# Spectral mixing followed by a squared-ReLU FFN: batch 0 and the filter loaded over all 128 partitions, products of batch 0 summed in TensorE, batch 1's steps moved to later slots

## The chip, the cores and the metric

The kernel runs on one core of a Trainium2 chip. The metric is device time of one execution in microseconds (us), median over several executions. A span that a trace gives is a little shorter than that time (846.0 against 848.0 for the kernel before), so times of kernels are compared with times and spans with spans. In this kernel TensorE does the matrix products and leaves them in PSUM; VectorE and ScalarE copy results out of PSUM ("evict" them), and with GpSimd cast, copy and multiply; SyncE and ScalarE issue the DMAs, the transfers between DRAM and the memory on chip, which the DMA engines carry out.

## The reference, cut to what matters

```python
# x (8, 3008, 256), filt_r and filt_i (1505, 256), w_in (256, 2048), w_out (2048, 256), all float32
X = np.fft.rfft(x, axis=1)
Y = X * (filt_r + 1j * filt_i)[None, :, :]
y = np.fft.irfft(Y, n=3008, axis=1).astype(np.float32)
h = np.maximum(y.reshape(24064, 256) @ w_in, 0.0)
out = (h * h @ w_out).astype(np.float32)
```

The length 3008 is split as 64 x 47. A forward transform is stage A (47-point sums, on the rows as they were loaded), a transposition through DRAM (`u` is written, `ut` read back), and stage B (64-point sums). VectorE multiplies the result by the filter. Stage P is the inverse 64-point step, `z` goes through DRAM, and stage Y is the inverse 47-point step. The feed-forward part (FFN) then takes 512 tokens at a time. I call one pass of its inner loop a **slot**. Batch 0's transform runs alone in a prologue; each later batch's transform is spread over the slots of the batch before it.

## The kernel before

Its prologue loads x of batch 0 over 94 of 128 partitions, in four chunks, and the filter in eight pieces, half of them with the rows in reverse order:

```python
    def load_f(k, im, rev, q):
        c0, c1 = 12 * k, 12 * k + 12
        r0 = 64 * im + 32 * rev
        v = (filt_i if im else filt_r)[0:1504, :].rearrange("(k1 k2) d -> k1 k2 d", k2=47)
        if rev:
            a = max(c0, 1)
            q.dma_start(out=f32s[k][r0:r0 + 32, a - c0:12, :], in_=v[:, 47 - a:47 - c1:-1, :])
        else:
            q.dma_start(out=f32s[k][r0:r0 + 32, :, :], in_=v[:, c0:c1, :])
```

One unit of stage B computes a product with the filter's real and imaginary parts, swaps the halves of the second one on GpSimd, adds, and gives the sum to stage P:

```python
        nc.vector.tensor_mul(out=prod, in0=ps..., in1=sF[:, :, 2 * p:2 * p + 2, :])
        yf = p_yf.tile([128, 2, D], F16, tag="yf", name=f"yf_{b}_{p}")
        swap = nc.gpsimd if b < 2 else nc.vector
        swap.tensor_copy(out=yf[0:64], in_=prod[64:128, 1])
        swap.tensor_copy(out=yf[64:128], in_=prod[0:64, 1])
    # unit_s:
        nc.vector.tensor_add(out=yf, in0=prod[:, 0], in1=yf)
    # ... (unit_p: two matmuls of yf with sSP, ScalarE evicts, z is written)
```

The write of `u` in the prologue is issued by ScalarE, and there are three `u` buffers for four chunks. The plan of batch 1 puts product and sum of unit p into slots 15 + p and 16 + p (the sum ahead of the next product on VectorE), the reads of z at slot 29, and stage Y from slot 32 on.

## Time and profile before

| | before |
|---|---|
| median of 3 executions | 848.01 us (847.49 to 848.17) |
| profiled span, mean granted TensorE clock | 846.0 us, 0.996 |
| TensorE busy, share of the span | 766.5 us, 91% |
| last eviction of stage P of batch 0 | 70.8 us |
| first FFN matmul | 83.58 us |
| slot 15, slot 30, slot 40 start | 110.40, 153.67, 181.17 us |

The last three rows are from the timeline. They divide the span into the parts that the change can touch: prologue, 15 slots with stage A of batch 1 (which it leaves alone), 15 slots with stage B of batch 1, 10 slots with z and Y of batch 1. What follows, from 181 us to the end, is 665 us that TensorE fills.

### The profile page before, as it was taken

To read this page: it belongs to the slowest core of one execution; us is meant where nothing else is said; L and a number is where in the kernel's file an instruction comes from. 1 tells how busy PE (TensorE), PEld (TensorE's weight loads), DVE (VectorE), ACT (ScalarE), POOL (GpSimd) and SP (SyncE) were. 2 spreads that over 40 slices of the span, in tenths; PEclk is the share of its full clock that TensorE was granted. 3 is DMA by queue.
4 is the path that set the end of the run, shared out by engine and by line. 5 is a ranking of instruction groups with operands and counts; after the bars stand their busy time and mean duration, and the time that the engine had idled before them with its cause. 6 is when DMAs were issued, how large, how long until landed. Compare 5 with 4: busy or idle time off the path is not lost.

```text
span 846.0 us, 13875 instructions
## 1 busy us (share of the span) xinstructions
PE 766.5 (91%) x5760; PEld 531.1 (63%) x5760; DVE 550.4 (65%) x876; ACT 548.7 (65%) x694; POOL 54.2 (6%) x66
## 2 busy tenths in 40 slices
PE   3224887699999999999999999999999999999998
PEld 0112454476677767677767767677767767676666
DVE  4444766455995579755995579755995579543332
ACT  2323755476777767776777767776777767766663
POOL 1186034000000000000000000000000000000000
PEclk9999999899999999999999999999999999999999
DMA  9946544625454245715453345715543332411111
GB/s 242 329 183 169 156 142 126 175 63 169 141 145 115 84 146 149 208 44 169 144 144 112 90 142 153 201 45 167 148 137 114 91 141 75 132 38 39 38 38 50
DMA packets 90799, 109.86 MB, mean 130 GB/s; under 512 B 4120, under 2 KB 80888, under 8 KB 86264
## 3 DMA queue, kind: packets, MB, share of 16 engines
q1 hardware_dynamic: 82256, 100.32, 39.6%
q10 hardware_dynamic: 8384, 8.62, 3.7%
q8 instruction: 45, 0.74, 0.4%
q14 instruction: 18, 0.15, 0.1%
q0 software_dynamic: 96, 0.04, 0.0%
HBM read 59.15 MB, written 49.81 MB: 129 GB/s over the span
## 4 chain that ended last, share of the span: by engine, by line
PE 82%; DMA 7%; DVE 4%; POOL 3%; issue 1%; ACT 1%; ACTq 0%; POOLq 0%; DVEq 0%; SPq 0%
PE psO L371 37%; PE psH L356 36%; DVE prod L275 3%; PE psA L234 3%; PE psY L326 2%; PE psP L298 2%; PE psB L272 2%; DMA f<-in_filt_i_dram 2%; DMA dZ<-ze 1%; POOL yf L281 1%; DMA x<-in_x_dram 1%; POOL yf L282 1%; POOL sF L446 1%; PE psA L252 1%; DMA sSA<-cSA 1%
## 5 line engine op out<-in xcount | busy, mean ns | idle before, releaser
L360 ACT ACTIVATE h<-psH 128x1024 f16<-128x1024 f32 x376 | 384.9, 1024 | 194.1 <-PE psH L356 192.4
L371 PE MATMUL psO<-sWout,h 128*128 128x256 f16 x3008 | 389.5, 273 | 0.0
L356 PE MATMUL psH<-yt,sWin 128*128 128x512 f16 (+7 forms) x1728 | 387.9, 352 | 0.7 <-ACT h L360 0.3
L371 PEld LDWEIGHTS <-h 128*128 128x128 f16 x3008 | 291.3, 98 | 77.2 <-issue 0.6
L364 DVE TENSOR_TENSOR h<-h 128x1024 f16<-128x1024 f16 x376 | 254.2, 685 | 106.0 <-ACT h L360 105.7
L356 PEld LDWEIGHTS <-sWin 128*128 128x128 f16 x1728 | 160.0, 98 | 103.7 <-issue 5.1
L275 DVE TENSOR_TENSOR prod<-psB,sF 128x1024 f16<-128x1024 f32 x96 | 116.9, 1219 | 4.7 <-PE psB L272 4.0
L300 ACT CAST ze<-psP 128x512 f16<-128x512 f32 x96 | 56.2, 585 | 53.9 <-PE psP L298 51.9
L335 DVE CAST yt<-psY 128x376 f16<-128x376 f32 x64 | 35.1, 549 | 69.7 <-PE psY L326 69.4
L241 DVE CAST u<-psA 96x512 f16<-96x512 f32 x56 | 38.4, 686 | 47.8 <-PE psA L234 47.7
L298 PE MATMUL psP<-yf,sSP 128*128 128x256 f16 x192 | 39.5, 290 | 26.9 <-DVE yf L288 15.9
L288 DVE TENSOR_TENSOR yf<-prod,yf 128x512 f16<-128x512 f16 x96 | 40.8, 425 | 30.7 <-POOL yf L282 28.0
L378 ACT COPY ost<-psO 128x512 f32<-128x512 f32 x94 | 55.4, 590 | 6.8 <-PE psO L371 6.0
L326 PE MATMUL psY<-sSY,zt 96*128 96x94 f16 x512 | 43.2, 215 | 13.3 <-DMA zt<-dZ 13.2
L272 PE MATMUL psB<-ut,sSB 128*128 128x256 f16 x192 | 39.0, 289 | 17.9 <-DMA ut<-dU 11.9
L326 PEld LDWEIGHTS <-zt 96*128 96x128 f16 x512 | 36.4, 104 | 29.6 <-DMA zt<-dZ 15.4
L219 DVE CAST x<-x 94x2048 f16<-94x2048 f32 (+1 forms) x36 | 39.2, 1098 | 10.8 <-DMA x<-in_x_dram 10.8
L272 PEld LDWEIGHTS <-sSB 128*128 128x128 f16 x192 | 19.6, 102 | 41.6 <-issue 17.6
L234 PE MATMUL psA<-x,sSA 94*96 94x512 f16 x112 | 42.3, 382 | 2.1 <-DVE u L241 1.3
L298 PEld LDWEIGHTS <-sSP 128*128 128x128 f16 x192 | 17.3, 100 | 36.1 <-DVE yf L288 18.9
L333 ACT CAST yt<-psY 128x376 f16<-128x376 f32 x64 | 29.8, 468 | 14.1 <-PE psY L326 7.4
L239 ACT CAST u<-psA 96x512 f16<-96x512 f32 x56 | 32.1, 574 | 0.0
(28 smaller groups left out, 143.4 us busy)
## 6 DMA issues: line engine op xcount, KB each, us to landing
out_dram<-ost SPq DMA_DIRECT2D x94, 256.0 KB, 3.7
x<-in_x_dram SPq DMA_DIRECT2D x26, 768.0 KB, 6.1
dU<-u SPq DMA_DIRECT2D x28, 384.0 KB, 3.4
dZ<-ze SPq DMA_DIRECT2D x28, 384.0 KB, 2.7
zt<-dZ SPq DMA_DIRECT2D x28, 384.0 KB, 4.6
ut<-dU SPq DMA_DIRECT2D x8, 1024.0 KB, 5.9
ut<-dU SPq DMA_DIRECT2D x8, 512.0 KB, 3.9
x<-in_x_dram SPq DMA_DIRECT2D x4, 640.0 KB, 6.0
```

The costliest lines, as they stand in the source:

```text
L234: nc.tensor.matmul(ps[0:96, :], sSA, x16s[(b, c)][:, 2 * i:2 * i + 2, :], start=True, stop=True)
L272: nc.tensor.matmul(ps[:, i * D:(i + 1) * D], sSB[:, 2 * p + i, :], uts[b][:, 2 * p + i, :], start=True, stop=True)
L275: nc.vector.tensor_mul(out=prod, in0=ps.rearrange("p (a d) -> p a d", d=D).unsqueeze(1).to_broadcast([128, 2, 2, D]), in1=sF[:, :, 2 * p:2 ...
L288: nc.vector.tensor_add(out=yf, in0=prod[:, 0], in1=yf)
L298: nc.tensor.matmul(ps[:, i * D:(i + 1) * D], sSP[:, 2 * p + i, :], prod[:, i, :], start=True, stop=True)
L300: nc.scalar.copy(out=zes[(b, c)][:, 2 * i6:2 * i6 + 2, :], in_=ps.rearrange("p (a d) -> p a d", d=D))
L326: nc.tensor.matmul(ps[:, 94 * jj:94 * jj + 94], zt[:, 4 * (g % 2) + jj, dt * 128:(dt + 1) * 128], sSY, start=True, stop=True)
L356: nc.tensor.matmul(ps[:, i, o:o + n], sWin[:, dt, jt * 128:(jt + 1) * 128], yts[b][:, dt, r:r + n], start=(dt == 0), stop=(dt == 1))
L360: nc.scalar.activation(out=h2[:, 2 * s:2 * s + 2, :], in_=ps, func=AF.Relu)
L364: nc.vector.tensor_mul(out=v, in0=v, in1=v)
L371: nc.tensor.matmul(pso[g][:, t % 2, :], h2s[g][:, jt, t * 128:(t + 1) * 128], sWout[:, jt, :], start=(jt == 0), stop=(jt == NJT - 1))
L378: nc.scalar.copy(out=ost, in_=pso[g])
```

## The change

Its intent is a shorter prologue and a batch 1 in which VectorE no longer waits for GpSimd. x of batch 0 comes in three loads over all 128 partitions in rows of 8 KB (a second set of stage-A weights sorts this out). Each filter part comes in one load of 128 partitions with rows of 12 KB, and casts on ScalarE, GpSimd and VectorE put the pieces into place. In batch 0 the swap and the sum vanish: stage P accumulates both products in PSUM with two weight sets. In batch 1 the sum moves behind the slot's second matmul group, and P, z and Y one slot later.

```diff
-    load_f(0, 1, 0, nc.scalar)        # ... and seven more, reversed rows among them
+    for k, filt in enumerate((filt_r, filt_i)):
+        t = p_y.tile([128, 12, D], F32, tag="yt", name=f"f32_{k}")
+        src = bass.AP(tensor=filt.tensor, offset=filt.offset,
+                      ap=[[12 * D, 4], [47 * D, 32], [1, 12 * D]])
+        nc.sync.dma_start(out=t, in_=src)
...
+                for v, w in enumerate((sSP, sSPx[0])):        # unit_p, b == 0
+                    nc.tensor.matmul(ps[:, i * D:(i + 1) * D], w[:, c2, :], prod[:, v, i, :],
+                                     start=(v == 0), stop=(v == 1))
...
-            put(r + (b == 1), 0, unit_s, b, p)
-            put(r + 2, 1, unit_p, b, p)
+            put(r + (b == 1), b == 1, unit_s, b, p)
+            put(r + 2 + (b == 1), 1, unit_p, b, p)
...
-            put(29 if b == 1 else 35, 1, read_z, b, c)
+            put(30 if b == 1 else 35, 1, read_z, b, c)
-            put((32 if b == 1 else 39) + n // 2, n % 2, unit_y, b, n)
+            if b == 1:
+                r, k = divmod(n, 3) if n < 6 else divmod(n - 2, 2)
+                put(33 + r, min(k, 1), unit_y, b, n)
+            else:
+                put(39 + n // 2, n % 2, unit_y, b, n)
```

More of the change, by code (lines that the diff above doesn't have):

```diff
@@ L31, in _build_consts @@
             SA[:, h, h, 1, c] = np.sin(2 * np.pi * n2 * c / N2)
+    S0 = np.zeros((128, 6, 2, 48))
+    for h in range(2):
+        q = SA[:, h, h].reshape(N2, 48)
+        for t in range(2):
+            S0[2 * h + t::4, t, h] = q[:32]
+        for c in range(4):
+            S0[4 * h + c:120:8, 2 + c, h] = q[32:]
     freq = np.full((NC, 64), -1)
@@ L39, in _build_consts @@
                 freq[c, 32 + j] = 47 * j + 47 - c
-    freq[0, 32] = N // 2
+    freq[0, 63] = N // 2
     SB = np.zeros((NM, 2, 2, NC, 2, 64))
@@ L57, in _build_consts @@
                 SB[:, h, 1, c, 1, f] = -sg * np.cos(th)
-            if c == 0 and f == 32:
+            if c == 0 and f == 63:
                 SB[:, :, 1, c, :, f] = 0.0
@@ L77, in _build_consts @@
     f16 = lambda a, p: np.ascontiguousarray(a.reshape(p, -1).astype(np.float16))
-    return f16(SA, 94), f16(SB, 128), f16(SP, 128), f16(SY, 96)
+    C0 = np.zeros((128, 864))
+    C0[:, 0:576] = S0.reshape(128, 576)
+    C0[0:94, 576:672] = SA.reshape(94, 96)
+    C0[0:96, 672:766] = SY.reshape(96, 94)
+    return f16(C0, 128), f16(SB, 128), f16(SP, 128)
 @with_exitstack
@@ L100 @@
     assert NG * TG == T
-    SA_np, SB_np, SP_np, SY_np = _build_consts()
-    dSA = nc.inline_tensor(SA_np, name="cSA")
+    C0_np, SB_np, SP_np = _build_consts()
+    dC0 = nc.inline_tensor(C0_np, name="cC0")
     dSB = nc.inline_tensor(SB_np, name="cSB")
     dSP = nc.inline_tensor(SP_np, name="cSP")
-    dSY = nc.inline_tensor(SY_np, name="cSY")
     const = ctx.enter_context(tc.tile_pool(name="const", bufs=1))
@@ L154, in load_x @@
         x32s[(b, c)] = t
-    sSA = const.tile([94, 96], F16, name="sSA")
-    nc.gpsimd.dma_start(out=sSA, in_=dSA.ap())
+    sC0 = const.tile([128, 864], F16, name="sC0")
+    nc.scalar.dma_start(out=sC0, in_=dC0.ap())
+    s0 = sC0[:, 0:576].rearrange("p (w q) -> p w q", q=96)
+    sSA = sC0[0:94, 576:672]
+    sSY = sC0[0:96, 672:766]
+    x0 = []
+    v0 = xrows[0:2048, :].rearrange("(p m) d -> p m d", m=16)
+    v1 = xrows[2048:3072, :].rearrange("(p m) d -> p m d", m=8)
+    for k, v in enumerate((v0[:, 0:8, :], v1, v0[:, 8:16, :])):
+        t = (p_h2 if k == 2 else p_x32).tile([128, 8, D], F32, tag="h2" if k == 2 else "x32",
+                                             name=f"x0_{k}")
+        nc.sync.dma_start(out=t, in_=v)
+        x0.append(t)
@@ L161 @@
+    f32s = []
+    for k, filt in enumerate((filt_r, filt_i)):
[3 more added lines that the diff above has]
+        nc.sync.dma_start(out=t, in_=src)
+        f32s.append(t)
     sSB = const.tile([128, NC, 128], F16, name="sSB")
+    nc.sync.dma_start(out=sSB, in_=dSB.ap().rearrange("p (a b) -> p a b", b=128))
     sSP = const.tile([128, NC, 128], F16, name="sSP")
-    sSY = const.tile([96, 94], F16, name="sSY")
+    nc.sync.dma_start(out=sSP, in_=dSP.ap().rearrange("p (a b) -> p a b", b=128))
@@ L166 @@
     sF = const.tile([128, 2, NC, D], F16, name="sF")
-    f32s = [p_y.tile([128, 12, D], F32, tag="yt", name=f"f32_{k}") for k in range(2)]
-    nc.gpsimd.memset(f32s[0][32:64, 0, :], 0.0)
-    nc.gpsimd.memset(f32s[0][96:128, 0, :], 0.0)
-    nc.gpsimd.dma_start(out=f32s[0][32:33, 0, :], in_=filt_r[1504:1505, :])
-    nc.gpsimd.dma_start(out=sSY, in_=dSY.ap())
-    def load_f(k, im, rev, q):
-        c0, c1 = 12 * k, 12 * k + 12
-        r0 = 64 * im + 32 * rev
-        v = (filt_i if im else filt_r)[0:1504, :].rearrange("(k1 k2) d -> k1 k2 d", k2=47)
-        if rev:
-            a = max(c0, 1)
-            q.dma_start(out=f32s[k][r0:r0 + 32, a - c0:12, :], in_=v[:, 47 - a:47 - c1:-1, :])
-        else:
-            q.dma_start(out=f32s[k][r0:r0 + 32, :, :], in_=v[:, c0:c1, :])
@@ L183, with cast_f @@
-    load_x(0, 0)
-    load_f(0, 1, 0, nc.scalar)
-    load_x(0, 1)
-    load_f(0, 1, 1, nc.scalar)
-    load_x(0, 2, p_h2, "h2")
-    load_x(0, 3, p_h2, "h2")
-    load_f(0, 0, 0, nc.sync)
-    load_f(0, 0, 1, nc.sync)
-    nc.sync.dma_start(out=sSB, in_=dSB.ap().rearrange("p (a b) -> p a b", b=128))
+    def cast_f(im, q, eng):
+        o = 64 * im + 32 * (q // 2)
+        c0 = (0, 12, 12, 0)[q]
+        src = f32s[im][32 * q:32 * q + 32, :, :]
+        if q >= 2:
+            src = src[:, ::-1, :]
+        dst = sF[o:o + 32, im, c0:c0 + 12, :]
+        if eng is nc.scalar:
+            eng.mul(out=dst, in_=src, mul=-1.0 if im else 1.0)
+        elif im:
+            eng.tensor_scalar_mul(out=dst, in0=src, scalar1=-1.0)
+        else:
+            eng.tensor_copy(out=dst, in_=src)
@@ L193, with cross_f @@
+    def cross_f(im, k):
+        c = slice(12 * k, 12 * k + 12)
+        if im:
+            nc.vector.tensor_scalar_mul(out=sF[0:64, 1, c, :], in0=sF[64:128, 1, c, :],
+                                        scalar1=-1.0)
+        else:
+            nc.vector.tensor_copy(out=sF[64:128, 0, c, :], in_=sF[0:64, 0, c, :])
     sWin = const.tile([128, 2, DFF], F16, name="sWin")
@@ L213, with cast_x @@
     x16s, us, uts, prods, zes, zts, yts = {}, {}, {}, {}, {}, {}, {}
-    def cast_x(b, c, parts=1):
+    def cast_x(b, c):
         t = p_x16.tile([94, 8, D], F16, tag="x16", name=f"x16_{b}_{c}")
-        n = 8 // parts
-        for k in range(parts):
-            nc.vector.tensor_copy(out=t[:, n * k:n * k + n, :],
-                                  in_=x32s[(b, c)][0:94, n * k:n * k + n, :])
-        x32s.pop((b, c))
+        nc.vector.tensor_copy(out=t, in_=x32s.pop((b, c))[0:94])
         x16s[(b, c)] = t
@@ L243, in unit_a, with chunk_a0 @@
             write_u(b, c, nc.sync)
-    def chunk_a(b, c):
-        us[(b, c)] = p_u.tile([96, 8, D], F16, tag="u", name=f"u_{b}_{c}")
+    def chunk_a0(c):
+        us[(0, c)] = p_u.tile([96, 8, D], F16, tag="u", name=f"u_0_{c}")
         for k in range(2):
-            ps = psH(f"psA_{b}_{c}_{k}")
+            ps = psH(f"psA_0_{c}_{k}")
             for i in range(2):
-                m = 4 * k + 2 * i
-                nc.tensor.matmul(ps[0:96, i, :], sSA, x16s[(b, c)][:, m:m + 2, :],
-                                 start=True, stop=True)
-            o = us[(b, c)][:, 4 * k:4 * k + 4, :]
+                m = slice(4 * k + 2 * i, 4 * k + 2 * i + 2)
+                nc.tensor.matmul(ps[0:96, i, :], s0[:, c // 2, :], x016[2 * (c % 2)][:, m, :],
+                                 start=True, stop=False)
+                nc.tensor.matmul(ps[0:96, i, :], s0[0:120, 2 + c, :], x016[1][0:120, m, :],
+                                 start=False, stop=True)
+            o = us[(0, c)][:, 4 * k:4 * k + 4, :]
             pv = ps[0:96].rearrange("p t (a d) -> p (t a) d", d=D)
@@ L259, in chunk_a @@
                 nc.vector.tensor_copy(out=o, in_=pv)
-        write_u(b, c, nc.scalar)
+        write_u(0, c, nc.scalar)
     def read_u(b):
@@ L278, in unit_b @@
             in1=sF[:, :, 2 * p:2 * p + 2, :])
-        yf = p_yf.tile([128, 2, D], F16, tag="yf", name=f"yf_{b}_{p}")
-        swap = nc.gpsimd if b < 2 else nc.vector
-        swap.tensor_copy(out=yf[0:64], in_=prod[64:128, 1])
-        swap.tensor_copy(out=yf[64:128], in_=prod[0:64, 1])
-        prods[(b, p)] = prod, yf
+        prods[(b, p)] = prod
+        if b > 0:
+            yf = p_yf.tile([128, 2, D], F16, tag="yf", name=f"yf_{b}_{p}")
+            swap = nc.gpsimd if b == 1 else nc.vector
+            swap.tensor_copy(out=yf[0:64], in_=prod[64:128, 1])
+            swap.tensor_copy(out=yf[64:128], in_=prod[0:64, 1])
+            prods[(b, p)] = prod, yf
     def unit_s(b, p):
@@ L289, in unit_s @@
         prods[(b, p)] = yf
+    sSPx = []
     def unit_p(b, p):
@@ L297, in unit_p @@
         for i in range(2):
-            nc.tensor.matmul(ps[:, i * D:(i + 1) * D], sSP[:, 2 * p + i, :], prod[:, i, :],
-                             start=True, stop=True)
+            c2 = 2 * p + i
+            if b == 0:
+                for v, w in enumerate((sSP, sSPx[0])):
+                    nc.tensor.matmul(ps[:, i * D:(i + 1) * D], w[:, c2, :], prod[:, v, i, :],
+                                     start=(v == 0), stop=(v == 1))
+            else:
+                nc.tensor.matmul(ps[:, i * D:(i + 1) * D], sSP[:, c2, :], prod[:, i, :],
+                                 start=True, stop=True)
         nc.scalar.copy(out=zes[(b, c)][:, 2 * i6:2 * i6 + 2, :],
@@ L413, in fft_plan @@
         for n in range(16):
-            put((32 if b == 1 else 39) + n // 2, n % 2, unit_y, b, n)
+            if b == 1:
+                r, k = divmod(n, 3) if n < 6 else divmod(n - 2, 2)
+                put(33 + r, min(k, 1), unit_y, b, n)
+            else:
+                put(39 + n // 2, n % 2, unit_y, b, n)
         return plan
@@ L419, in run, with cast_x0 @@
             f(*a)
-    for c in range(4):
-        cast_x(0, c, 2)
-        chunk_a(0, c)
+    x016 = [p_x16.tile([128, 8, D], F16, tag="x16", name=f"x016_{k}") for k in range(3)]
+    def cast_x0(k, i, copy):
+        m = slice(4 * i, 4 * i + 4)
+        copy(out=x016[k][:, m, :], in_=x0[k][:, m, :])
+    for k in range(2):
+        for i in range(2):
+            cast_x0(k, i, nc.vector.tensor_copy)
+    chunk_a0(0)
+    chunk_a0(2)
+    for i in range(2):
+        cast_x0(2, i, nc.scalar.copy)
@@ L425 @@
+    chunk_a0(1)
+    chunk_a0(3)
     read_u(0)
-    for im in range(2):
-        for rev in range(2):
-            load_f(1, im, rev, nc.scalar)
-    nc.sync.dma_start(out=sSP, in_=dSP.ap().rearrange("p (a b) -> p a b", b=128))
     load_w()
-    nc.scalar.copy(out=sF[0:64, 0, 0:12, :], in_=f32s[0][0:64])
-    nc.vector.tensor_scalar_mul(out=sF[64:128, 1, 0:12, :], in0=f32s[0][64:128], scalar1=-1.0)
-    nc.vector.tensor_scalar_mul(out=sF[0:64, 1, 0:12, :], in0=sF[64:128, 1, 0:12, :], scalar1=-1.0)
@@ L434 @@
-    nc.vector.tensor_copy(out=sF[64:128, 0, 0:12, :], in_=sF[0:64, 0, 0:12, :])
-    for r in range(15):
+    for q in (0, 3):
+        cast_f(0, q, nc.scalar)
+    for q in (1, 2):
+        cast_f(0, q, nc.gpsimd)
+    for q in (0, 3):
+        cast_f(1, q, nc.vector)
+    for q in (1, 2):
+        cast_f(1, q, nc.scalar)
+    sSPx.append(p_x32.tile([128, NC, 128], F16, tag="x32", name="sSPx"))
+    for k in range(2):
+        c = slice(12 * k, 12 * k + 12)
+        nc.gpsimd.tensor_copy(out=sSPx[0][0:64, c, :], in_=sSP[64:128, c, :])
+        nc.gpsimd.tensor_copy(out=sSPx[0][64:128, c, :], in_=sSP[0:64, c, :])
@@ L436 @@
+    for k in range(2):
+        for im in range(2):
+            cross_f(im, k)
+    for r in range(14):
         if r < 12:
             unit_b(0, r)
-        if 1 <= r < 13:
-            unit_s(0, r - 1)
-        if r >= 3:
-            unit_p(0, r - 3)
-        if r in (1, 3):
-            h = r // 2
-            nc.scalar.copy(out=sF[64 * h:64 * h + 64, 0, 12:24, :], in_=f32s[1][0:64])
-        if r == 1:
-            nc.gpsimd.tensor_scalar_mul(out=sF[64:128, 1, 12:24, :], in0=f32s[1][64:128],
-                                        scalar1=-1.0)
@@ L448 @@
-        if r == 4:
-            nc.vector.tensor_scalar_mul(out=sF[0:64, 1, 12:24, :], in0=sF[64:128, 1, 12:24, :],
-                                        scalar1=-1.0)
+        if r >= 2:
+            unit_p(0, r - 2)
+    cast_w()
     for c in range(4):
@@ L454 @@
         load_x(1, c, q=nc.scalar)
-    cast_w()
     for n in range(16):
```

## The prediction

> **What bounds the kernel now.** I read the page first, its 40 slices above all.
>
> ```profile
> span 846.0 us, 13875 instructions
> PE   3224887699999999999999999999999999999998
> DMA  9946544625454245715453345715543332411111
> ```
>
> A slice is 21 us. From the ninth on (170 us) TensorE is 90% busy or more: nothing in the change can shorten that part. All that can be won lies in the first eight slices: the prologue (batch 0's transform, TensorE 20 to 40% busy) and the first forty slots of the feed-forward, which also carry batch 1's transform. Next I read the chain of waits in order of time, for the prologue:
>
> ```profile
> 20.58 1.95 PE psA L252 x4
> ...
> 30.18 13.91 DMA f<-in_filt_i_dram
> 44.13 0.13 issue
> 44.26 7.96 POOL sF L446
> 52.23 0.05 issue
> ...
> 53.90 1.22 DVE prod L275
> ```
>
> Columns: start, duration, what. The filter's second half lands at 44.1, and then GpSimd takes 7.96 us to cast it, with its swaps for stage B queued behind. The timeline adds the rest: stage A runs from 9.0 to 23.8; the intermediate read back (ut) lets stage B start at 34.47; the first five products are out by 40.8, then VectorE idles 12.7 us; in the settled part a product and its sum take 1.58 us a unit; the last eviction of stage P ends at 70.8; the feed-forward starts at 83.58. So the end of P fixes the start of the feed-forward, 12.8 us later.
>
> Then the views by stretches, for the DMA (last two numbers: busy share of the 16 engines, GB/s):
>
> ```profile
> 12.00:14.00 2.00, 1.12 (x3) 0.59 (x4) 1.42 (x3) 0.00 (x0) 0.00 (x0) 1.00 1.04 274
> 46.00:48.00 2.00, 0.00 (x0) 0.00 (x0) 0.00 (x0) 0.00 (x0) 2.00 (x1) 1.00 1.09 387
> ```
>
> The queues are saturated in both, but rows of 1 KB in reverse order beside 8 KB ones give 274, the plain weights 387 (24.2 per engine). Last, the timeline of TensorE and VectorE in the batch-1 stage:
>
> ```profile
> 116.61 1.03 PE L356 MATMUL psH<-yt,sWin 128*128 128x512 f16 x4
> 119.70 0.39 PE L298 MATMUL psP<-yf,sSP 128*128 128x256 f16 x2 [0.97 <-DVE prod L275]
> 119.93 1.03 PE L356 MATMUL psH<-yt,sWin 128*128 128x512 f16 x4
> 121.39 0.43 DVE L288 TENSOR_TENSOR yf<-prod,yf 128x512 f16<-128x512 f16 x1 [1.16 <-POOL yf L282]
> 157.14 1.03 PE L356 MATMUL psH<-yt,sWin 128*128 128x512 f16 x4
> 163.78 0.49 PE L326 MATMUL psY<-sSY,zt 96*128 96x94 f16 x4 [5.61 <-DMA zt<-dZ]
> ```
>
> L356 marks each slot's start. Slots here take 3.31 us (116.61 to 119.93) though TensorE's own work is 2.2: VectorE waits in order for GpSimd's swap before the next product. Later TensorE waits 5.61 us for the read of z.
>
> **What the Trainium skill says.** (1) "DMA: Bandwidth & Descriptors", section "Why a DMA increments its semaphore by 16 and not by 1": a DMA runs on the largest k up to 16 engines that divides the outermost dimension of both its access patterns. The new filter load has a hand-made source pattern whose outermost dimension is 4 (12 rows x 32 x 4). So it gets **four engines, not sixteen**. Nothing in the trace of before shows a large load with such a shape. (2) Same page, "Queues, rings and completion order": every engine serves its queues in turn, packet by packet. The trace agrees: the first write of u, issued at 12.31 beside filled queues, is still awaited at 22.09, while the last, issued at 23.91, had landed by 27.6. (3) "TensorE: Matmul & The Clock Gate", "Back-to-back issue gap": columns/1.2 ns cold, columns/2.4 plus 2.5 ns warm. The trace agrees: 512 columns are 0.43 us apart in stage A and 0.22 in the feed-forward.
>
> **The change part by part.**
>
> *x of batch 0* over 128 partitions: the same 3.1 MB in rows of 8 KB. At an estimated 365 GB/s (between 350 and 389 seen from 40 to 50 us) it has landed by 12 instead of about 18.
>
> *Stage A* needs 32 matmuls instead of 16: cold 8 x 0.43 = 3.4 us a chunk, in place of the 3.86 us that VectorE's cast, wait and eviction cost. Start near 9.7, end near 26 if nothing blocks it. No gain. But there are three u buffers: the fourth chunk waits for the first write of u.
>
> *Filter on four engines.* Each of these moves 3.15 MB / 4 = 786 KB of it; at an estimated 25 GB/s (24.2 was seen per engine) 31.4 us. After x at 11.0 that gives 42.4, with u's packets in between 44. Behind it in the ring lie sSB and sSP (98 KB per engine, 4 us) and the rest of u's writes (135 rows per engine, estimated at 27 ns each: a write of u in the quiet batch-1 stage lands in 3.1 us, some 1.3 of it for 48 rows; 3.6 us): 51.7. Receipt 1.5, read of ut 3.5: stage B can start at 56.7; if the writes get through early and the read queues directly, at 54.6. I take **56**. The casts end close by: ScalarE is held by chunk four until some 41, then four casts at 2.75 us and a cross copy on VectorE: 53.5.
>
> *Stages B and P* lose the 12.7 us stall, the swaps and the sum. VectorE needs 1.17 us a unit (two products took 2.35). TensorE needs two B and four P matmuls of 256 columns, 1.29 us cold, half of it warm. Five units cold and seven at VectorE's pace: 6.5 + 8.2 = 14.6, plus 1.3 for the last P and eviction: 15.9 us instead of 36.3. P ends at 56 + 15.9 = 71.9 against 70.8. **Prologue: 1.1 us later.** The gain of the quicker B is spent on the filter that arrives later. The w casts lie beside that; the weights (behind ut, about 16 us) are there by 70 and cast by 75.
>
> *Batch 1* is the real gain. The sum moves behind the second matmul group of its slot, so the product no longer stands behind the swap. A swap takes about 1.7 us from the product's end (0.94 + 0.61 and gaps), and its sum comes a slot of 2.2 us later. VectorE's own work per slot is 1.14 + 0.34 + 0.60 = 2.1 us by start-to-start distances, below TensorE's 2.2. Slots 15 to 29: before 110.40 to 153.67 = 43.3 us; after, 3 at 1.96, 9 at 2.2 and 3 at 1.96: 31.7. Saved 11.6. Slots 30 to 39: before 153.67 to 181.17 = 27.5. After: ten slots at 1.735, 16 Y units at 0.165, and a remaining wait: z's write, now clear of the x load, lands 3.8 us after slot 30 starts, its read 3.3 later, so 7.3 with issue, against 6.1 at which Y wants it: 1.2 to 1.5. Sum 21.5, saved 6.0. Allowing a little for VectorE at 95%: **17 us saved**.
>
> Sum: 848.0 - 17 + 1.1 = 832.1; I say 832.5.
>
> **The rivals.** *A: the filter does run on all engines.* For it: the author must have meant it so. Then 9.6 MB are in by 29 us, ScalarE's 11 us of casts become the wait before B (the fourth chunk waits for u until about 27, casts to 39), B starts at 40.5, P ends at 56.4, and the total is 848 - 17 - 14.4 = 817. Against it: the rule above; I give 12%. *B: four engines do worse than 24 to 25 GB/s each, or the starved u writes take longer.* At 20 GB/s the filter takes 39 us and B starts at 64: 840. Nothing in the profile speaks on four engines alone; 15%. *C: VectorE and GpSimd get into each other's way in batch 1.* The swap's first half takes 0.94 to 1.01 us beside VectorE and 0.60 alone; two VectorE operations now fall beside it, so that it could come to 1.4 and the sum would just wait. Slots at 2.6 instead of 2.2 give back 5 us: 837. *D: four-engine rate at the top (27 GB/s) and u through early:* B at 53, 829.
>
> **Range and chances.** Main branch 832.5 with a spread of about 4 (rate of an engine, remaining wait for z), and 12% near 817. The 2% line is 831.05, just below the main branch, so this is close: faster 0.42, same 0.56, slower 0.02. Range 818 to 839.
>
> **What would show it.** In the changed profile: DMA share of 0.25 to 0.4 from about 15 to 42 us with near 100 GB/s (four engines of sixteen); the filter loads taking over 12 us each; the fourth chunk's eviction waiting for a u write until nearly 40; stage B from about 56 and 1.2 to 1.3 us a unit without GpSimd; feed-forward start at 85 against 83.6; slots 18 to 26 at 2.2 us; TensorE waiting for z under 2 us. I am wrong if the share stays near 1 until B starts (then rival A), if B's units take over 1.4 us, or if the batch-1 slots still wait for GpSimd.

## The result, and the profile after

The changed kernel takes **852.88 us** (median of 4, 851.58 to 854.47) against 847.84 us for the kernel before on the same chip. The ratio is 1.006, 95% interval 1.0038 to 1.0082: within 2%, but slower, not faster. Ratios here are the mean time of one kernel's fast runs over that of the other's of the same rounds, so they are not quite the ratio of the medians that I quote.

The first view of the page, the one with 40 slices of 21 us, for the kernel after:

```profile
span 849.5 us, 13895 instructions
PE   3105699899999999999999999999999999999998
DMA  9328955545455245815455235815454242511111
```

Before, the DMA row began 9946; now it begins 932. In the second and third slices the DMA engines are busy for 30 and 20% of the time, and TensorE for 10 and 0%. The time went there. The view by stretches of the changed kernel says how much moved (after the stretch's length come busy us of PE, PEld, DVE, ACT and POOL, then clock, DMA share, GB/s):

```profile
10.00:12.00 2.00, 1.95 (x5) 0.97 (x5) 0.60 (x1) 0.47 (x1) 0.00 (x0) 1.00 1.13 369
28.00:32.00 4.00, 0.00 (x0) 0.00 (x0) 0.00 (x0) 0.00 (x0) 0.00 (x0) 0.50 0.27 86
44.00:48.00 4.00, 0.00 (x0) 0.00 (x0) 0.00 (x0) 0.00 (x0) 0.00 (x0) 0.50 0.26 102
```

A share of 0.26 is four engines of sixteen. The chain of waits in order of time (start, duration, what) shows what that cost:

```profile
14.55 38.93 DMA dU<-u
...
54.91 2.02 ACTq L255
...
56.98 2.76 ACT sF L213
59.75 2.77 ACT sF L213
...
68.17 0.95 DVE sF L222
69.15 1.94 DVE prod L307 x2
```

The first write of u is out for 38.93 us. The fourth chunk needs its buffer and can't be evicted before it. Only after that does ScalarE come to its four filter casts, VectorE to the cross copies, and the products start at **69.15**. ScalarE's timeline adds a detail (an ACTq row is the engine's sequencer at an issue of a DMA):

```profile
23.01 16.48 ACTq L255 DMA_DIRECT2D dU<-u  x1
53.56 1.01 ACT L289 CAST u<-psA 96x1024 f16<-96x1024 f32 x1 [32.26 <-DMA dU<-u]
```

The issue of the third write alone held ScalarE's sequencer for 16.48 us, where the first two took 0.35 and 0.32.

For batch 1, VectorE's timeline in a slot of the kernel before (first three lines) and of the kernel after (next four):

```profile
118.42 1.22 DVE L275 TENSOR_TENSOR prod<-psB,sF 128x1024 f16<-128x1024 f32 x1
119.56 0.68 DVE L364 TENSOR_TENSOR h<-h 128x1024 f16<-128x1024 f16 x1
121.74 1.22 DVE L275 TENSOR_TENSOR prod<-psB,sF 128x1024 f16<-128x1024 f32 x1
```

```profile
142.53 1.21 DVE L307 TENSOR_TENSOR prod<-psB,sF 128x1024 f16<-128x1024 f32 x1
143.66 0.41 DVE L322 TENSOR_TENSOR yf<-prod,yf 128x512 f16<-128x512 f16 x1
144.00 1.09 DVE L406 TENSOR_TENSOR h<-h 128x1024 f16<-128x1024 f16 x1
145.01 1.21 DVE L307 TENSOR_TENSOR prod<-psB,sF 128x1024 f16<-128x1024 f32 x1
```

Product to product was 3.32 us and is 2.48. The wait for the swap is gone, but VectorE is now busy without a gap: the FFN's square (`h<-h`) takes 1.09 us instead of 0.68. Later, TensorE (first line) and SyncE's issues at the read of z:

```profile
168.50 0.50 PE L368 MATMUL psY<-sC,zt 96*128 96x94 f16 x4 [3.85 <-DMA zt<-dZ]
```

```profile
157.12 0.33 SPq L163 DMA_DIRECT2D x<-in_x_dram  x1
157.54 0.39 SPq L422 DMA_DIRECT2D out_dram<-ost  x1
159.23 0.32 SPq L346 DMA_DIRECT2D dZ<-ze  x1
164.56 2.38 SPq L353 DMA_DIRECT2D zt<-dZ  x4
```

From the start of each part in both timelines (slots counted by their first-group matmuls: in the kernel after, slot 15 starts at 124.22, slot 30 at 158.42, slot 40 at 185.24) comes this account of the profiled spans:

| part | before, us | after, us | difference |
|---|---|---|---|
| prologue, up to the first FFN matmul | 83.58 | 97.69 | +14.1 |
| slots 0 to 14 | 26.82 | 26.53 | -0.3 |
| slots 15 to 29 (stage B of batch 1) | 43.27 | 34.20 | -9.1 |
| slots 30 to 39 (z and Y of batch 1) | 27.50 | 26.82 | -0.7 |
| the rest | 664.83 | 664.26 | -0.6 |
| span | 846.0 | 849.5 | +3.5 |

Batch 1 gained 10 us in all, nearly all of it in stage B, and the prologue lost 14.

### The profile page after: what moved, and what is told of

It reads as the page before. It is cut to its first block, busy times and chain, and to the rows that moved or that the text cites. A ratio compares the mean times of both kernels' runs of the same rounds, so it can differ in the third digit from the quotient of the medians.

```text
span 849.5 us, 13895 instructions
## 1 busy us (share of the span) xinstructions
PE 770.7 (91%) x5800; PEld 538.7 (63%) x5800; DVE 552.1 (65%) x862; ACT 553.9 (65%) x697; POOL 40.6 (5%) x42
## 4 chain that ended last, share of the span: by engine, by line
PE 84%; DMA 7%; DVE 4%; issue 2%; ACT 2%; ACTq 0%; SPq 0%; DVEq 0%
PE psO L413 38%; PE psH L398 37%; DMA dU<-u 5%; PE psA L264 3%; PE psY L368 2%; PE psB L304 2%; PE psP L340 2%; DVE prod L307 2%; DMA zt<-dZ 1%; DMA x<-in_x_dram 1%; ACT h L402 1%; ACT sF L213 1%; DVE yf L322 0%; DVE sF L225 0%; DVE sF L222 0%
## 5 line engine op out<-in xcount | busy, mean ns | idle before, releaser
L406 DVE TENSOR_TENSOR h<-h 128x1024 f16<-128x1024 f16 x376 | 258.9, 697 | 107.6 <-ACT h L402 107.2
L368 PE MATMUL psY<-sC,zt 96*128 96x94 f16 x512 | 43.2, 217 | 12.0 <-DMA zt<-dZ 12.0
L264 PE MATMUL psA<-x,sC 94*96 94x512 f16 x112 | 42.3, 382 | 0.8 <-ACT u L269 0.6
L322 DVE TENSOR_TENSOR yf<-prod,yf 128x512 f16<-128x512 f16 x84 | 35.5, 423 | 3.0 <-POOL yf L316 0.5
L251 DVE CAST x<-x 94x2048 f16<-94x2048 f32 x28 | 34.1, 1217 | 2.1 <-DMA x<-in_x_dram 2.1
L289 ACT CAST u<-psA 96x1024 f16<-96x1024 f32 x4 | 4.0, 1007 | 44.6 <-DMA dU<-u 32.3
L340 PE MATMUL psP<-yf,sSP 128*128 128x256 f16 x168 | 32.1, 273 | 0.0
```

Source lines behind the costliest of these rows:

```text
L264: nc.tensor.matmul(ps[0:96, :], sSA, x16s[(b, c)][:, 2 * i:2 * i + 2, :], start=True, stop=True)
L340: nc.tensor.matmul(ps[:, i * D:(i + 1) * D], sSP[:, c2, :], prod[:, i, :], start=True, stop=True)
L368: nc.tensor.matmul(ps[:, 94 * jj:94 * jj + 94], zt[:, 4 * (g % 2) + jj, dt * 128:(dt + 1) * 128], sSY, start=True, stop=True)
L406: nc.vector.tensor_mul(out=v, in0=v, in1=v)
```

## The experiments

**Theory.** The filter loads run on four engines because the outermost dimension of their source pattern is 4; everything in the prologue hangs on that. **First rival:** the prologue is late for another reason (u's writes starved by packets of 12 KB, the three u buffers, ScalarE as a bound). For batch 1, **theory:** the square is slowed by GpSimd's copies, and z waits in the ring (the queue of the issuing engine) behind an x load; **rival:** the new order of the plan itself.

### e1: the same filter bytes on all engines

```diff
-        src = bass.AP(..., ap=[[12 * D, 4], [47 * D, 32], [1, 12 * D]])
-        nc.sync.dma_start(out=t, in_=src)
+        for qq in range(4):
+            src = bass.AP(tensor=filt.tensor, offset=filt.offset + 12 * D * qq,
+                          ap=[[47 * D, 32], [1, 12 * D]])
+            nc.sync.dma_start(out=t[32 * qq:32 * qq + 32], in_=src)
```

> The changed kernel with each filter load cut into four loads of 32 partitions, so that the outermost dimension of both access patterns is 32 instead of 4; same bytes, same queue, same order. Theory (four engines carry the filter): the DMA share stays near 1 until the loads are in, the filter has landed by 25 us instead of 55.9, the first write of u lands before 30 instead of 53.5, stage B's products start near 41 instead of 69.15 (bound now by ScalarE's casts), feed-forward starts near 70 instead of 97.7, total about 825 us (820 to 832). Rival (it is the amount: the whole filter, in 12 KB rows, is put ahead of u and ut on the queue, on however many engines): the write of u stays starved, stage B starts after 55, total 838 or more.

Measured: **822.75 us** (before 847.2 on the same chip), ratio 0.9702 [0.9682, 0.9722]. Same bytes, same rows, same casts. The view of this kernel by stretches and VectorE's timeline:

```profile
20.00:24.00 4.00, 3.63 (x9) 1.79 (x9) 0.03 (x1) 2.27 (x3) 0.93 (x1) 1.00 1.03 278
41.04 13.67 DVE L308 TENSOR_TENSOR prod<-psB,sF 128x1024 f16<-128x1024 f32 x12
```

The share is about 1, the products start at 41.04 instead of 69.15, the FFN at 69.62. The shape of the access pattern alone costs the change 28 us at the first product and 30 us in all. The theory stands, with the numbers it gave for the products, the FFN and the total.

### e12: a dose for the rule

The same loads cut in two halves with an outermost dimension of 2.

```diff
+        for qq in range(2):
+            src = bass.AP(tensor=filt.tensor, offset=filt.offset + 24 * D * qq,
+                          ap=[[12 * D, 2], [47 * D, 32], [1, 12 * D]])
+            nc.sync.dma_start(out=t[64 * qq:64 * qq + 64], in_=src)
```

> A dose for the rule of the outermost dimension: the changed kernel with each filter load cut in two halves whose source pattern has an outermost dimension of 2 (same bytes, same rows). If the outermost dimension sets the number of engines, both halves run on the same two engines: after x the DMA share falls to about 0.13 (2 of 16) and the rate to about 30 to 52 GB/s, the filters are in only near 85 to 95 us instead of 56, and the time is about 885 to 895 us. If the four engines of the changed kernel had another cause (the rows, the length of the queue), two loads of half the size would be no slower: share 0.25 or more and about 853 us.

Measured: 876.53 us (one run, state unknown; before 847.18). In its view by stretches:

```profile
20.00:30.00 10.00, 4.31 (x12) 1.88 (x10) 1.22 (x1) 0.99 (x1) 0.00 (x0) 0.67 0.13 38
```

0.13 is two engines of sixteen. ScalarE's casts found the third half landed at 69.1 and the fourth at 84.4. That is 15.3 us for 393 KB per engine, or 25.7 GB/s per engine. The products started at 94.3. The time is some 10 us under the 885 to 895 that I expected, the filters' landing at the early end of it. In its first stretch, 20 to 30 us, each of the two moved 19 GB/s. With e1 this gives three points (16, 4 and 2 engines: 823, 853, 877 us) and settles the cause of the late prologue.

### e5: u's writes on SyncE's queue, behind the filters

```diff
-        write_u(0, c, nc.scalar)
+        write_u(0, c, nc.sync)
```

> The changed kernel, filter still on four engines, with batch 0's writes of u issued on SyncE's queue, behind the filter loads, instead of on ScalarE's queue beside them. Theory (each 512 B row of u that is served in turn between two 12 KB filter rows costs far more than my 27 ns, some 0.25 us, so the mixing stretched the filter from about 43 to 55.9 us): the filter has landed by 44 (43 to 46), u follows in one go, stage B's products start near 62 instead of 69.15, total about 846 (843 to 849). Rival (an engine that moves 12 KB rows for four engines simply gives 18 GB/s, with u beside it or not): the filter lands after 52, products start at 70 or later, total 853 or more.

Measured: 853.24 us, ratio 1.0056 [1.0028, 1.0083]. My idea that u's rows, mixed in between, stretched the filter load fell: the cast that waits for the first filter part still starts at 37.6, as with u beside it, and the packets in the kept traces put the last filter row at 52.7 (55.3 with u): 3 us, not 12. The two stretches show that the rate on four engines changes with time, with next to nothing else in flight:

```profile
28.00:32.00 4.00, 0.00 (x0) 0.00 (x0) 0.00 (x0) 0.00 (x0) 0.00 (x0) 0.50 0.24 77
44.00:48.00 4.00, 0.00 (x0) 0.00 (x0) 0.00 (x0) 0.00 (x0) 0.00 (x0) 0.50 0.25 104
```

77 GB/s is 19 per engine, 104 is 26. The second filter part went at the rate that I had used; the first didn't.

### e9 and e11: the imaginary part first

```diff
-    for k, filt in enumerate((filt_r, filt_i)):
+    for k, filt in ((1, filt_i), (0, filt_r)):
```

e9 does this on four engines, e11 on sixteen (on top of e1).

> The changed kernel with the two filter loads in the other order (imaginary part first), still on four engines. In the changed kernel the first filter took about 25 us after x, the second about 17. Theory 1, the position counts (whatever is loaded first, in the time just after x, is slow): the imaginary part lands near 37, the real part near 56, the time stays at 852 to 853. Theory 2, the source itself counts (the real part is slow to read wherever it stands): the imaginary part lands near 29, and the real part near 54 to 56.

> The version with the filters in quarters (sixteen engines), with the imaginary part first. Its use is the rate of the first and of the second filter load. If position counts, 12 to 20 us again shows about 200 GB/s at a full share and the time stays at 822 to 824; if the source counts, the first load is done sooner (before 15 us) and the second later than in the other order.

Measured: e9 852.95 us, ratio 1.0064 [1.0028, 1.01]; e11 824.18 us (one run, state unknown). In e9 the rates from 24 to 40 us are 55 to 74 GB/s and from 44 to 60 us 83 to 97; the real part, now second, landed at 60.8 (the profiled execution was the slowest of e9's four, 858.07 us). In e11 the stretches from 12 to 20 us show 212 and 206 GB/s at a full share, in e1 218 and 198. The source does not count. Nor does the place in the order by itself: in e1 the second part was no faster than the first (232, 215 and 184 GB/s in the 2 us stretches from 22 to 28, against 203, 234 and 215 from 12 to 18), and in e5 the rate rises through both parts (68, 77, 83, 92, 104, 104 GB/s in the 4 us stretches from 24). What fits all of these runs is the time since x. Why a load is slow in that time stays **open**: the bytes and the row length are the same.

### e2 and e6: a fourth buffer for u

e2, a fourth buffer in u's own pool, didn't build: the memory on chip didn't suffice. e6 takes a buffer that is idle in the prologue instead.

```diff
-        us[(0, c)] = p_u.tile([96, 8, D], F16, tag="u", name=f"u_0_{c}")
+        us[(0, c)] = (p_zt if c == 3 else p_u).tile([96, 8, D], F16,
+                          tag="zt" if c == 3 else "u", name=f"u_0_{c}")
```

> The changed kernel, filter still on four engines, with the fourth chunk of u put into a free buffer of the z pool, so that its eviction waits for no write. It stands for the run with four u buffers, which did not fit. Theory (the block on the u buffer holds ScalarE in order and so sets the last casts, but the read of ut would be late anyway): fourth chunk evicted by 27 us instead of 53.6, ScalarE's real-part casts at 37 to 43, filter still landing near 56, ut near 65, products start near 65.5 instead of 69.15, total about 849 (847 to 851). Rival (the u buffer was the whole loss): products start before 58, total under 843.

Measured: 852.83 us, ratio 1.0056 [1.0034, 1.0079]: no gain, and neither theory nor rival had the reason. ScalarE's timeline:

```profile
25.86 14.53 ACTq L255 DMA_DIRECT2D dU<-u  x1
40.43 1.01 ACT L290 CAST u<-psA 96x1024 f16<-96x1024 f32 x1 [16.57 <-issue]
41.47 17.71 ACTq L255 DMA_DIRECT2D dU<-u  x1
59.23 11.09 ACT L213 ACTIVATE sF<-f 32x3072 f16<-32x3072 f32 x4 [17.79 <-issue]
```

The fourth chunk waits for no buffer now: VectorE's half of its eviction runs at 27.15, ScalarE's at 40.4, 13 us earlier. But the third and the fourth issue of a u write hold ScalarE for 14.53 and 17.71 us, and the casts stand behind them in ScalarE's order: two of the four had had their data since 39.0 us, and all four run from 59.23 on, later than in the changed kernel (56.98). The products start at 71.41.

### e10: both, so that nothing holds ScalarE

e5 and e6 together.

> The changed kernel with u's writes issued by SyncE behind the filters and a fourth buffer for the fourth chunk of u: nothing on ScalarE waits for a queue and no chunk waits for a buffer. Theory: both together free ScalarE, so its last two filter casts start when the second filter lands (about 54) and are over by 60, and the products then start at what is left, the landing of ut. If ut can't land before 64 (u lies behind the filter on four engines), the products start near 66 and the time is about 848 to 850, so that the bytes on four engines set the rest; rival: ut lands by 60 and the time falls to 843 to 845, so that the blocked ScalarE was the larger part.

Measured: 851.51 us (before 848.57), ratio 1.003 [0.9996, 1.0063]. ScalarE and VectorE's lines of this kernel:

```profile
56.39 5.53 ACT L213 ACTIVATE sF<-f 32x3072 f16<-32x3072 f32 x2 [11.46 <-DMA f<-in_filt_i_dram]
69.47 13.67 DVE L308 TENSOR_TENSOR prod<-psB,sF 128x1024 f16<-128x1024 f32 x12 [2.17 <-PE psB L305]
```

ScalarE is done at 61.9 and all casts and cross copies by 67.3; SyncE's issue of the u writes takes the blocking (39.66 us for two). The products wait for ut alone, and start at 69.47 against 69.15. The theory's kind was right and its number 3 us too early. So in the changed kernel two chains end within 2.7 us: the casts behind a blocked ScalarE (69.1) and ut behind the bytes on four engines (landed at 66.4). Freeing one leaves the other. Of what was tried, only the number of engines moves both.

### e3: the plan of batch 1 alone, in the kernel before

The last three parts of the diff above, in the kernel before.

> The kernel before with the change's batch-1 schedule alone (sum moved behind the second matmul group, P one slot later, read of z one slot later, Y packed into seven slots); the loads, the filter and batch 0 as before. Theory (the two stages are independent, and the batch-1 part earns 10 us that the prologue loses again): feed-forward starts at 83.6 as before, slots 18 to 26 take 2.49 us instead of 3.31, total about 838 (836 to 840.5). Rival (the batch-1 gain in the changed kernel comes from its later start or from fewer transfers beside it): 843 or more.

Measured: 836.93 us, ratio 0.9874 [0.9855, 0.9893], with the FFN starting at 84.06. The plan of batch 1 is worth 10.3 us by itself. Taken from e1's gain of 24.5 it leaves 14.2 for the prologue, and the FFN did start 14.0 us earlier in e1: the parts add up.

### e4: without GpSimd's swaps in batch 1

```diff
-            swap.tensor_copy(out=yf[0:64], in_=prod[64:128, 1])
-            swap.tensor_copy(out=yf[64:128], in_=prod[0:64, 1])
+            if b > 1:
+                swap.tensor_copy(out=yf[0:64], in_=prod[64:128, 1])
+                swap.tensor_copy(out=yf[64:128], in_=prod[0:64, 1])
```

The sum takes the unswapped product in batch 1, so that VectorE's work stays the same and the result of batch 1 is wrong (relative error 0.37).

> Wrong result on purpose: the changed kernel without GpSimd's two swap copies in batch 1; the sum takes the product's second half directly, same shape. Theory (GpSimd's copies slow VectorE's square down, 1.09 us beside them instead of 0.69, and that sets the pace): square back at 0.69 in these slots, slots 18 to 26 at 2.2 us instead of 2.49, total 2 to 3 us under the changed kernel, about 850. Rival (VectorE's own order and its three operations set the pace): slots stay at 2.4 to 2.5 and the square keeps over 1 us.

Measured: 843.32 us against 852.88 for the changed kernel (another chip of the same type; before 847.2 there, ratio 0.9969 [0.9929, 1.0008]). A slot of it:

```profile
142.14 0.69 DVE L407 TENSOR_TENSOR h<-h 128x1024 f16<-128x1024 f16 x1
142.84 1.22 DVE L307 TENSOR_TENSOR prod<-psB,sF 128x1024 f16<-128x1024 f32 x1
```

The square is back at 0.69, a slot (product to product) at 2.17 us, which is the 2.2 of my prediction. The 0.4 us of the square is thus GpSimd's doing. It seems to matter which starts first: in the kernel before, too, a copy of the swap lies beside the square, but there the square started 0.14 us ahead of it (119.56), took 0.68, and the copy took 1.01; in the changed kernel the copy starts 0.13 us ahead of the square (144.00), and takes 0.67, the square 1.09. Slots 15 to 29 gained 2.7 us, as expected. Slots 30 to 39 gained 4.6 us more, which I had not expected, and 1.9 of the rest is a prologue that happened to be shorter. The 4.6 came from z: TensorE waited 1.85 us for it instead of 3.85, and its clock stayed up.

### e7: x of batch 2 loaded after z

That pointed to the x load. e7 is e1 with the last two x loads of that batch issued after the reads of z, and the casts that need them later.

```diff
-                put(27 + 3 * c, 1, cast_x, b + 1, c)
+                put(27 + 3 * c if not late or c < 2 else 33 + 2 * c, 1, cast_x, b + 1, c)
-                    put(27 + 3 * c, 1, load_x, b + 1, c + 2)
+                    put(30 + c if late else 27 + 3 * c, 1, load_x, b + 1, c + 2)   # late = (b == 1)
```

> The run with the filter on 16 engines, with batch 2's second pair of x loads moved behind the read of z (slots 30 and 31), their casts three slots later. Theory (z's last write stands in the ring behind a 786 KB x load and a 256 KB output, which makes TensorE wait 3.6 us for z and drops its clock): z's write lands in under 3.5 us instead of about 5, TensorE's wait for z under 1.5 us, no stretch at the low clock after it, total 3 to 5 us less, near 818.5. Rival (the write and read of z are that slow by themselves): wait stays over 3 us, total 821 or more.

Measured: **817.1 us**, ratio 0.9636 [0.9616, 0.9655], 5.6 us under e1 (822.75; between two chips whose kernels before differ by 0.7). TensorE and SyncE:

```profile
130.43 0.32 SPq L347 DMA_DIRECT2D dZ<-ze  x1
132.86 2.15 SPq L354 DMA_DIRECT2D zt<-dZ  x4
136.53 0.34 PE L369 MATMUL psY<-sC,zt 96*128 96x94 f16 x4 [0.68 <-DMA zt<-dZ]
```

From the last write of z to the issue of its read takes 2.4 us. Over the kernels this interval goes with the head start of the x load: issued 0.9 us ahead of the write, it is 6.7 us (before); 2.1 ahead, 5.0 to 5.3 (e3, e1, after); 3.9 ahead, 3.5 (e4); not ahead, 2.4 (e7). So the write of z is late because of the x load that was issued just before it; whether that is their order in the ring or the shared DMA engines, no run here separates. Slots 30 to 39 take 20.9 us, against 26.4 in e1: that is the gain. This version beats both kernels.

### e8: more on top of e7

The third x tile cast on GpSimd, one filter cast on VectorE, and e6's buffer.

> A version to beat both: the previous run, plus x's third tile cast on GpSimd instead of ScalarE, one of ScalarE's four filter casts given to VectorE between two chunks, and the fourth u buffer. Theory (with the filter on 16 engines, stage B waits for ScalarE's 11 us of casts and for ut, which both hang on the end of stage A): stage A's last write of u leaves at 24 instead of 28, products start near 36 instead of 41, total about 814 (811 to 817). Rival (B is bound by the bytes that have to come in first): products start no earlier than 40, total that of the previous run.

Measured: 817.58 us, ratio 0.9642 [0.9623, 0.9661]: nothing over e7. The products start at 39.66 instead of 40.34, when ut has landed (39.0). The edit missed its own aim: stage A's last write of u left at 27.4, not at 24 (25.9 in e7), because VectorE's new filter cast (19.6 to 23.1) stood before an eviction. So it is not shown that the bytes bound the prologue on sixteen engines, as the rival said.

## Why the prediction was wrong

The prediction was 832.5 us, and the range ended at 839. The result of 852.9 is outside. The miss is 20.4 us: 13.0 in the prologue (+14.1 instead of +1.1), 7 in batch 1 (-10.0 instead of -17), the rest in neither.

**Four engines: right.** It was read from the pattern with the Trainium skill ("DMA: Bandwidth & Descriptors", section "Why a DMA increments its semaphore by 16 and not by 1"); the share of 0.26, e1 and e12 agree.

**"At an estimated 25 GB/s (24.2 was seen per engine) 31.4 us": this step failed by its size.** The filter was to be in at 44; it was in at 55.9. x was through at about 12, where the rate falls from 369 to 184 GB/s; the first part had landed by 37.6, some 26 us for 393 KB per engine, an estimated 15 GB/s. The second took 18.3 us, 21 GB/s. The 24.2 came from a stretch in which all sixteen engines moved plain weights, and it holds for the second part alone (26 in e5). A hint was there: the 274 GB/s at 12 to 14 us in the kernel before, which I put down to reversed rows. No rows are reversed after the change, and the same stretch shows 184 GB/s at a full share.

**"The fourth chunk waits for the first write of u", until some 40: the wait was right, its end wrong.** It ended at 53.5, within 2.4 us of the second filter part. I had u's packets take turns with the filter's, and they do: from 22 to 40 us the kept trace has 113 filter rows of 12 KB and 117 rows of u. Each of the four engines has 48 rows of that write, so it waits for about as many filter rows: the end fails with the rate above. e5 and e6 show that neither u's queue nor the buffer alone is at fault.

**"I take 56" for ut and 53.5 for the casts: the two that follow from it.** ut landed at 66.4, and the casts and cross copies ended at 69.1. The casts' own 11.1 us were as I had them (4 x 2.77). What I left out is that an issue can hold its engine: 16.48, 14.53 and 17.71 us on ScalarE. It didn't cost more than ut did (e10), but it made e6 useless.

**Stages B and P: right.** 15.9 us were predicted, from 69.15 to the last eviction at 84.2 there are 15.05 (TensorE's first matmuls of stage B ran at 66.49 already and then stood waiting for the casts). The swap-free batch 0 does what it was made for.

**Batch 1: the mechanism right, two terms mis-sized.** The product no longer stands behind the swap. "VectorE's own work per slot is 1.14 + 0.34 + 0.60 = 2.1 us": the square's term was 1.0 (start to start, 144.00 to 145.01), so that VectorE became the bound at 2.48 us a slot and 11.6 became 9.1 us (the fifteen slots took 34.2 us, not 31.7; in e4, with the square at 0.69, 31.5). This is my rival C, whose mechanism e4 shows, though the square grew rather than the swap, and the slot took 2.48 and not 2.6. The Trainium skill had it ("SBUF — State Buffer", section "SBUF: two separate sides": the port pair that VectorE and GpSimd share is an exclusive lock, and a VectorE operation with two inputs in SBUF is named among those that block), and I had not drawn on it. The second term, "z's write, now clear of the x load", failed: it was not clear, the load was issued 2.1 us ahead of it. TensorE waited 3.85 us and ran at half its clock for a while after (one group of four FFN matmuls took 1.91 us, 1.03 otherwise). 6.0 became 0.7 us, which is the larger half of batch 1's miss; e7 gets it (20.9 us for these ten slots, 6.6 saved).

**The chances.** Rivals B (slower engines, 15%) and C stood as alternatives, with 840 and 837. They are independent, and both came. Added to the main branch (832.5 + 7.5 + 4.5) they make 844.5, and the range should have reached beyond that. "Same" had the highest chance (0.56) and came, but it stood for a kernel 1.8% faster and came as one 0.6% slower: luck.

## What to carry to other kernels

Read the outermost dimension of a DMA's two access patterns before anything else: the same 3.1 MB cost 30 us more with a 4 there than in four loads with a 32. Where a long load takes every second turn of a few DMA engines, the writes beside it land late, and the issue of a further one can hold its engine (16.48 us here), so an engine with work on the path should not issue there. And where work is moved to lie beside other work, look at which pairs share a port: a term of 0.6 us beside GpSimd was 1.0 once GpSimd started first.

## What the Trainium skill lacked or had wrong

- "DMA: Bandwidth & Descriptors", section "Why a DMA increments its semaphore by 16 and not by 1": nothing wrong; the rule for k holds here at 4 (share 0.26) and 2 (share 0.13). Its "Specifications" give one rate for an engine, about 27 GiB/s. Here one of two engines moved 25.7 GB/s as the mean of a whole load (e12) and one of four 26 at best, but only 14 to 19 from 24 to 32 us, whichever source it read and on two engines as on four (e5, e9, e12). No page that I read explains that, and no run here does.
- The same page, "Queues, rings and completion order", tells how engines take turns between rings. It doesn't say that an issue on a ring with much ahead of it can hold the issuing engine; "Perfetto Trace Analysis", section "DMA Instruction — HWDGE (DVE, Sync)", has an issue last until its descriptors are made, and gives no duration. ScalarE's sequencer was held for 16.48 us (after), 14.53 and 17.71 us (e6), each time with earlier writes of u still out; that these are the reason is inferred.
- "SBUF — State Buffer", section "SBUF: two separate sides": the lock agrees with the trace, and a number can be added. A square of 128x1024 f16 took 0.69 us without GpSimd's copies (e4) and 1.09 beside two copies of 64x512 f16, of which the second took 0.97 us against 0.67 for the first.
